# Building fp32 weights from double-precision bits: three VectorE passes after two ScalarE activations, instead of five passes after one

## The chip, the core and the metric

The kernel runs on one core of one Trainium2 chip. The metric is the device time of one execution, in microseconds. A core has five engines that run side by side and wait for one another by semaphores: TensorE (PE, matrix products; its weight loads are PEld), VectorE (DVE), ScalarE (ACT), GpSimd (POOL) and SyncE (SP, which here issues nearly all transfers). Each engine takes its own instructions in order.

## What is computed

An attention block with a delta rule feeds a gated feed-forward block. q, k and v have the shape (4, 8, 768, 48), in single precision; the three weights of the second block are in double precision.

```python
k_n = k / (np.linalg.norm(k, axis=-1, keepdims=True) + 1e-06)
for t in range(S):                       # S = 768
    y[:, :, t] = np.einsum('bhd,bhde->bhe', q[:, :, t], state)
    v_old = np.einsum('bhde,bhd->bhe', state, kt)
    state = state + bt[:, :, :, None] * np.einsum('bhd,bhe->bhde', kt, vt - v_old)
# x = y as 3072 tokens of 384
g = x @ w_gate                           # w_gate, w_val: 384 x 1536, w_out: 1536 x 384
silu = g * (1.0 / (1.0 + np.exp(-g)))
val = x @ w_val
out = (silu * val @ w_out).astype(np.float32)
```

The kernel works through the sequence in 12 chunks of 64 steps. Within a chunk the recurrence is a set of small matrix products and the inverse of a triangular matrix; the first such inverse is a substitution of 31 steps on VectorE, at the start of the kernel. After a chunk's attention part (called `advance`) its 256 tokens (`x_ffn`) go through the feed-forward block: `p_gate` and `p_val` are products with w_gate and w_val, `sil` is the silu of p_gate, `h_f` the product of sil and p_val, `p_o` the product with w_out.

The kernel multiplies in fp32. Each weight arrives as two 32-bit words, and the kernel makes an fp32 number of them. A double's high word holds the sign, 11 bits of exponent and the top 20 bits of mantissa; the low word holds the other 32 bits of mantissa. An fp32 number has 8 bits of exponent and 23 of mantissa.

## The kernel before

The weights are cut into 36 pieces of 128 rows. Pieces 0 to 11 are 256 wide (the first 512 columns of w_gate and w_val in turn, three row blocks each), 12 to 23 are 512 wide (the rest of both), 24 to 35 are 384 wide (w_out). Each piece is loaded into a place that some other tile owns until later (`h_f`, `zt`, `wo_sb`, or `staged`), converted, and only then is its place loaded again. This is the conversion. The L numbers in comments are those by which the profile names the lines; they were added here.

```python
def power_step(n):
    ...
    m = pieces[n][4]
    power = words(hp[10 + (n // 2 % 4 if n < N_HALF else (0, 2, 3, 1)[n % 4])])
    ...
    nc.vector.tensor_scalar(                       # L246: exponent bits of the high word
        out=power, in0=staged[n][:, :, 1],
        scalar1=0x7FF00000, scalar2=None, op0=ALU.bitwise_and,
    )
    nc.scalar.activation(                          # L254: exponent moved and rebiased
        power.bitcast(I32), power, ACTF.Relu, bias=rebias, scale=8.0
    )

def convert(ns):
    ...                                            # power_step for each of ns, if not yet done
    for dst, words, _ in work_of:
        nc.vector.tensor_scalar(                   # L266: top mantissa as an integer
            out=dst.bitcast(U32), in0=words[:, :, 1],
            scalar1=0xFFFFF, scalar2=1 << 20, op0=ALU.bitwise_and, op1=ALU.bitwise_or,
        )
    for dst, words, _ in work_of:
        nc.vector.scalar_tensor_tensor(            # L275: plus the low word, as fp32
            out=dst, in0=words[:, :, 0], scalar=2.0**-32, in1=dst.bitcast(U32),
            op0=ALU.mult, op1=ALU.add,
        )
    for n in range(ns[-1] + 1, ns[-1] + 7):
        if n < min(N_HALF, len(pieces)) or ns[-1] + 3 > n < len(pieces):
            power_step(n)                          # ahead, for later pieces
    for _, words, power in work_of:
        nc.vector.scalar_tensor_tensor(            # L287: the sign into the power of two
            out=power, in0=words[:, :, 1], scalar=0x80000000, in1=power,
            op0=ALU.bitwise_and, op1=ALU.bitwise_or,
        )
    for dst, _, power in work_of:
        nc.vector.scalar_tensor_tensor(            # L296: mantissa times power
            out=dst, in0=dst, scalar=2.0**-20, in1=power.bitcast(FP32),
            op0=ALU.mult, op1=ALU.mult,
        )
    for n in ns:
        for later in freed_by.get(n, ()):
            stage(later)                           # load the next piece into the freed place
```

The order of the start, as the kernel lists it (each engine gets its share in this order):

```python
for n, _ in enumerate(substitute(mb, zb)):   # DVE, L510 and L516
    if n == R // 2:
        for i in range(4):
            power_step(i)
m_1 = turned_m(1, "ffn")
scale_v_heads(0)                             # ACT, L396, 16 small activations
turned(1, True, "px")
for _ in late_z(0, zb):                      # DVE transposes into zt and d_t, L596 and L602
    pass
...
first_join = join_late(0, 0, ("px", "py"))
next(first_join)                             # PE p_j L620, ACT d_o L613 and t L622
converts(2)
next(first_q)                                # DVE p_sb, L459
next(first_join)                             # PE p_j L630, ACT zt L638
nc.scalar.copy(mb[:, m_1[0][0]], m_1[0][1])
step("advance", advance, 0)                  # PE p_u L763, ACT uu L774
converts(2)
step("advance", advance, 0)
nc.scalar.copy(mb[:, m_1[1][0]], m_1[1][1])
converts(2)
step("advance", advance, 0)                  # PE p_y, ACT y L815 and L817
converts(2)
step("advance", advance, 0)                  # PE p_f L827, ACT x_ffn L830
converts(2)
...
converts(2)
...
for c, f in pairs:                           # two 128-wide columns of w_gate and w_val each
    ...
    need((6, 12, 18, 18, 24, 24)[f // 2])    # pieces that must have been issued by then
    gate_val(c, f, fill, 1 if early else None)
need(len(pieces))
for bp in range(NB):
    point(2)
    output(0, bp, fill, (4, 8))              # PE p_o L876
```

`gate_val` issues p_gate (L847), sil (L856), a `fill`, p_val (L847), h_f (L862), a `fill`. While pieces remain, a `fill` converts the next piece (the first three fills the next two, and the first of them one more). `point` puts steps of the next chunk's attention part between: state (ACT L805), the second join (d_o, t, zt on ACT; p_j on PE), p_g (PE L444) and p_sb (DVE L459), p_r and p_y (PE L742, L751), the two passes on vin (DVE L401, L759), p_u (PE L763).

Of the kernel before, what the change touches and what calls it, by code (L numbers as in the profile page):

```python
# [7 lines left out]

FP32 = mybir.dt.float32
U32 = mybir.dt.uint32  # L10
I32 = mybir.dt.int32
ALU = mybir.AluOpType
ACTF = mybir.ActivationFunctionType

# [7 lines left out]
def kernel(  # L22
# [25 lines left out]
    nc = tc.nc  # L48
# [14 lines left out]
    const = ctx.enter_context(tc.tile_pool(name="const", bufs=1))  # L63
# [106 lines left out]
    load_k(0, (nc.sync, nc.scalar))  # L170
    load_k(1, (nc.sync, nc.scalar))
    beta_b = const.tile([128, NG, R], FP32, name="beta_b")
    rebias = const.tile([128, 1], FP32, name="rebias")
    nc.vector.memset(rebias, -896.0 * 2**23)
    wg_sb = const.tile([128, KT, DFF], FP32, name="wg_sb")
    wv_sb = const.tile([128, KT, DFF], FP32, name="wv_sb")
    wo_sb = const.tile([128, FT, DM], FP32, name="wo_sb")
# [3 lines left out]
    pieces = []  # L181
# [9 lines left out]
    staged, powers, places = {}, {}, {}  # L191

    def words(tile_):
        return tile_.bitcast(U32)
# [18 lines left out]
    for n, (name, lo) in enumerate(place_of):  # L213
        m = 2 * pieces[n][4]
# [10 lines left out]
    def stage(n):  # L225
        _, src, t, f0, m = pieces[n]
        name, lo = place_of[n]
        if name not in places:
            tag_bufs = {"zb": 1, "p_sb": 2}[name]
            places[name] = work.tile(  # L230
                [128, 2 * PIECE], U32, name="staged", tag=name, bufs=tag_bufs
            )
        place = places[name][:, lo : lo + 2 * m]
        staged[n] = place.rearrange("p (f two) -> p f two", two=2)
        nc.sync.dma_start(
            out=place, in_=src[t * 128 : (t + 1) * 128, f0 : f0 + m].bitcast(U32)
        )

    def power_step(n):
        if n in powers or n not in staged:  # L240
            return
        m = pieces[n][4]
        power = words(hp[10 + (n // 2 % 4 if n < N_HALF else (0, 2, 3, 1)[n % 4])])
        power = power[:, n % 2 * m : n % 2 * m + m] if n < N_HALF else power[:, 0:m]
        powers[n] = power
        nc.vector.tensor_scalar(  # L246
            out=power,
            in0=staged[n][:, :, 1],
            scalar1=0x7FF00000,
            scalar2=None,  # L250
            op0=ALU.bitwise_and,
        )

        nc.scalar.activation(  # L254
            power.bitcast(I32), power, ACTF.Relu, bias=rebias, scale=8.0
        )

    def convert(ns):

        work_of = []  # L260
        for n in ns:
            dst, _, t, f0, m = pieces[n]
            power_step(n)
            work_of.append((dst[:, t, f0 : f0 + m], staged.pop(n), powers.pop(n)))
        for dst, words, _ in work_of:
            nc.vector.tensor_scalar(  # L266
                out=dst.bitcast(U32),
                in0=words[:, :, 1],
                scalar1=0xFFFFF,
                scalar2=1 << 20,  # L270
                op0=ALU.bitwise_and,
                op1=ALU.bitwise_or,
            )
        for dst, words, _ in work_of:
            nc.vector.scalar_tensor_tensor(  # L275
                out=dst,
                in0=words[:, :, 0],
                scalar=2.0**-32,
                in1=dst.bitcast(U32),
                op0=ALU.mult,  # L280
                op1=ALU.add,
            )
        for n in range(ns[-1] + 1, ns[-1] + 7):
            if n < min(N_HALF, len(pieces)) or ns[-1] + 3 > n < len(pieces):
                power_step(n)
        for _, words, power in work_of:
            nc.vector.scalar_tensor_tensor(  # L287
                out=power,
                in0=words[:, :, 1],
                scalar=0x80000000,  # L290
                in1=power,
                op0=ALU.bitwise_and,
                op1=ALU.bitwise_or,
            )
        for dst, _, power in work_of:
            nc.vector.scalar_tensor_tensor(  # L296
                out=dst,
                in0=dst,
                scalar=2.0**-20,
                in1=power.bitcast(FP32),  # L300
                op0=ALU.mult,
                op1=ALU.mult,
            )
        for n in ns:
            for later in freed_by.get(n, ()):
                stage(later)
# [10 lines left out]
    for b in range(2):  # L317
        rows = mask_q[64 * b : 64 * b + 64]
        nc.gpsimd.affine_select(
            out=rows,  # L320
# [688 lines left out]
    def converts(n):  # L1009
        if todo:  # L1010
            convert(todo[:n])
            del todo[:n]
# [121 lines left out]
    with tc.manual_schedule(  # L1134
# [17 lines left out]
        for n in range(4):  # L1152
            stage(n)
# [3 lines left out]
        for n in range(4, 10):  # L1157
            stage(n)
# [32 lines left out]
        for n, _ in enumerate(substitute(mb, zb)):  # L1191
# [3 lines that stand above are left out]
# [102 lines left out]
```

## Time and profile before

| what | value |
|---|---|
| time, median of 3 runs | 738.45 us (738.15 to 738.98) |
| span of the profiled execution | 737.5 us |
| TensorE busy | 697.5 us, 95% |
| weight loads of TensorE busy | 604.7 us, 82% |
| VectorE busy | 473.1 us, 64% |
| ScalarE busy | 154.7 us, 21% |
| GpSimd busy | 66.9 us, 9% |
| bytes read from device memory | 31.01 MB |

The busy share is an average over stages with different limits, so it is read by stage: a line of 40 digits gives the busy tenths of each slice of 18.4 us, and a table of stretches gives busy microseconds. A timeline lists instructions by start time; the tile that is written stands left of the arrow, the tiles read right of it, then the shape and the count; a bracket at the end gives how long the engine had been idle before it and which instruction ended that. "Busy" counts an instruction's whole duration, and neighbours on VectorE and ScalarE overlap a little, so what one costs in a row is read from start to start. Conversions run from 33.6 us (the first L246) to 141 us (the last L296).

### The profile page before, as it was taken

What the parts mean: (1) busy time and instruction counts of PE and PEld (TensorE: products, weight loads), DVE (VectorE), ACT (ScalarE), POOL (GpSimd) and SP (SyncE); (2) the same over time, 40 slices, a digit from 0 to 9 for tenths busy, and PEclk for the clock granted to TensorE, in tenths of its full rate; (3) what the DMA queues carried; (4) which work ended last, traced back from release to release, by engine and by line L of the source; (5) the groups of instructions that cost most, each with busy time, mean ns of one, the idle gap of its engine ahead of it and who ended that gap; (6) DMA issues with size and microseconds to landing.
All of it is one profiled execution on the core that took longest, in us unless ns stands there. A gap on an engine that the chain in (4) does not pass through costs nothing.

```text
span 737.5 us, 22478 instructions
## 1 busy us (share of the span) xinstructions
PE 697.5 (95%) x10132; PEld 604.7 (82%) x10132; DVE 473.1 (64%) x977; ACT 154.7 (21%) x287; POOL 66.9 (9%) x46
## 2 busy tenths in 40 slices
PE   4657899999999999999999999999999999999997
PEld 3546788866787788988988988988988988989987
DVE  5999988978498163678854678854578853313122
ACT  3455443302401112011012011012011012021010
POOL 7008100201200000030000030000030000000000
PEclk9556999999999999999999999999999999999999
DMA  6775444121231012331302231302210100100000
GB/s 141 164 227 166 124 108 129 36 41 24 56 45 24 22 24 45 43 67 15 53 3 45 36 70 20 53 3 39 46 29 12 32 3 3 23 3 0 22 1 21
DMA packets 130735, 37.18 MB, mean 50 GB/s; under 512 B 122864, under 2 KB 125936, under 8 KB 130640
## 3 DMA queue, kind: packets, MB, share of 16 engines
q1 hardware_dynamic: 127184, 34.01, 22.7%
q10 hardware_dynamic: 3072, 1.57, 1.0%
q8 instruction: 79, 1.29, 0.7%
q0 software_dynamic: 384, 0.17, 0.1%
q14 instruction: 16, 0.13, 0.1%
HBM read 31.01 MB, written 4.72 MB: 48 GB/s over the span
## 4 chain that ended last, share of the span: by engine, by line
PE 83%; DVE 14%; issue 1%; DMA 1%; ACT 0%; ACTq 0%; SPq 0%; DVEq 0%
PE p_gate L847 23%; PE p_val L847 23%; PE p_o L959 17%; PE p_o L876 6%; DVE tmp L510 3%; PE p_g L444 3%; DVE zb L516 3%; PE p_u L763 2%; PE p_r L742 1%; PE p_s L794 1%; PE p_y L782 1%; PE p_y L751 1%; DVE last_h L287 1%; PE p_t L432 1%; DVE h_f L862 1%
## 5 line engine op out<-in xcount | busy, mean ns | idle before, releaser
L847 PE MATMUL p_gate<-x_ffn,wg_sb 128*128 128x256 f32 x864 | 204.4, 387 | 1.5 <-ACT x_ffn L830 1.5
L847 PE MATMUL p_val<-x_ffn,wv_sb 128*128 128x256 f32 x864 | 198.5, 379 | 0.0
L847 PEld LDWEIGHTS p_val<-x_ffn,wv_sb 128*128 128x128 f32 x864 | 163.8, 190 | 22.3
L847 PEld LDWEIGHTS p_gate<-x_ffn,wg_sb 128*128 128x128 f32 x864 | 161.1, 191 | 24.2 <-ACT x_ffn L830 2.0
L862 DVE TENSOR_TENSOR h_f<-sil,p_val 128x512 f32<-128x512 f32 x71 | 48.6, 684 | 147.5 <-PE p_val L847 147.0
L856 ACT ACTIVATE sil<-p_gate 128x512 f32<-128x512 f32 x72 | 43.0, 598 | 276.9 <-PE p_gate L847 247.3
L655 POOL TENSOR_TENSOR n_b<-mb,half 128x32 f32<-128x32 f32 x5 | 43.0, 8607 | 408.6 <-DVE mb L480 368.2
L959 PE MATMUL p_o<-wo_sb,h_f 128*128 128x192 f32 x432 | 75.6, 328 | 0.1
L959 PEld LDWEIGHTS p_o<-wo_sb,h_f 128*128 128x128 f32 x432 | 70.3, 190 | 1.2 <-DVE o_sb L969 0.7
L510 DVE TENSOR_TENSOR tmp<-zb,mb 128x31 f32<-128x31 f32 (+15 forms) x186 | 63.3, 340 | 12.2 <-PE p_j L630 6.8
L516 DVE TENSOR_TENSOR zb<-zb,tmp 128x31 f32<-128x31 f32 (+15 forms) x186 | 63.7, 343 | 6.5 <-DVE tmp L510 0.2
L969 DVE TENSOR_TENSOR o_sb<-o_sb,p_o 128x192 f32<-128x192 f32 x45 | 15.8, 350 | 53.4 <-PE p_o L959 36.2
L876 PE MATMUL p_o<-wo_sb,h_f 128*128 128x384 f32 x136 | 45.7, 490 | 0.0
L876 PEld LDWEIGHTS p_o<-wo_sb,h_f 128*128 128x128 f32 x136 | 25.3, 190 | 16.5
L959 PE MATMUL p_o<-last_k,h_f 128*128 128x192 f32 x180 | 32.2, 326 | 0.0
L959 PEld LDWEIGHTS p_o<-last_k,h_f 128*128 128x128 f32 x180 | 29.7, 190 | 0.0
L917 DVE TENSOR_TENSOR h_f<-h_f,h_f 128x256 f32<-128x256 f32 x54 | 22.4, 424 | 8.0 <-PE p_o L959 7.1
L959 PE MATMUL p_o<-last_h,h_f 128*128 128x192 f32 x144 | 26.3, 326 | 0.0
L959 PEld LDWEIGHTS p_o<-last_h,h_f 128*128 128x128 f32 x144 | 23.9, 190 | 0.0
L254 ACT ACTIVATE last_h<-last_h,rebias 128x512 int32<-128x512 uint32 (+2 forms) x26 | 15.3, 616 | 30.5 <-DVE last_h L246 30.4
L763 PEld LDWEIGHTS p_u<-vin,zt 64*64 64x64 f32 x768 | 13.7, 141 | 6.9 <-issue 3.2
L763 PE MATMUL p_u<-vin,zt 64*64 64x48 f32 x768 | 15.7, 228 | 2.4 <-DVE vin L759 1.2
(180 smaller groups left out, 692.6 us busy)
## 6 DMA issues: line engine op xcount, KB each, us to landing
vin<-in_v_dram SPq DMA_DIRECT2D x96, 48.0 KB
kn<-in_k_dram SPq DMA_DIRECT2D x40, 96.0 KB
out_dram<-o_sb SPq DMA_DIRECT2D x36, 96.0 KB
zt<-in_moe_w_out_dram SPq DMA_DIRECT2D x6, 384.0 KB
staged<-in_moe_w_out_dram SPq DMA_DIRECT2D x6, 384.0 KB
qpad<-in_q_dram SPq DMA_DIRECT2D x36, 64.0 KB
wo_sb<-in_moe_w_gate_dram SPq DMA_DIRECT2D x4, 512.0 KB
wo_sb<-in_moe_w_val_dram SPq DMA_DIRECT2D x4, 512.0 KB
```

Source lines behind the costliest of these rows:

```text
L444: nc.tensor.matmul(p_v[par][half_of(b if of_q else b ^ par), bp, j], kt[c][half_of(par), bp, j, b], xt[half_of(par), bp, j, b],)
L510: nc.vector.tensor_tensor(out=t_v, in0=zb[:, 0 : j + 1, j : j + 1].to_broadcast([128, j + 1, m]), in1=mb[:, j : j + 1, j + 1 : R].to_broad ...
L516: nc.vector.tensor_tensor(out=zb[:, 0 : j + 1, j + 1 : R], in0=zb[:, 0 : j + 1, j + 1 : R], in1=t_v, op=ALU.add,)
L655: nc.gpsimd.tensor_tensor(out=n, in0=mb.rearrange("p j i -> p (j i)")[:, 0 : R * R : R + 1], in1=half, op=ALU.pow,)
L763: nc.tensor.matmul(p_u[half_of(b), par, bp, j], zt[half_of(b ^ par), par, bp, j], r[half_of(b ^ par), par, bp, j], start=first, stop=True, ...
L847: nc.tensor.matmul(ps[name][:, i], w_sb[:, t, (f + i) * 128 : (f + i + 1) * 128], xts[c][:, t], start=(t == 0), stop=(t == KT - 1),)
L856: nc.scalar.activation(sil, ps[name], ACTF.Silu)
L862: nc.vector.tensor_tensor(out=hs[c, f], in0=sil, in1=ps["p_val"], op=ALU.mult)
L876: nc.tensor.matmul(p_o, hs[c, f - f % 2][:, f % 2, bp * 128 : (bp + 1) * 128], wo_sb[:, f], start=(f == 0), stop=(f == FT - 1),)
L917: nc.vector.tensor_tensor(out=out, in0=a, in1=b, op=ALU.subtract)
L959: nc.tensor.matmul(p[x, part], a(f - f % 2)[:, f % 2], b(f), start=not begun and f == 0, stop=f == FH - 1, skip_group_check=True,)
L969: nc.vector.tensor_tensor(out=out, in0=a, in1=b, op=ALU.add)
```

## The change

The exponent and the top mantissa are no longer taken apart. ScalarE reads the high word as if it were an fp32 number: its 8 exponent bits are then the upper 8 of the double's 11, and the lower 3 stand at the top of the mantissa. Multiplying by 2^-112 subtracts 112 from that exponent, so that a shift left by 3 then gives the exponent and the upper mantissa of the wanted fp32 number in place. A second activation multiplies the low word by 2^-29 and rounds it to an integer from 0 to 8: the last three bits of the mantissa, rounded. VectorE shifts the first result by three, puts the sign back (it lay in the bit that the shift pushed out), and adds the second result as an integer. So ScalarE has two activations per piece where it had one, with constants instead of a bias read from memory, and neither waits for a VectorE pass on the same piece; VectorE has three passes where it had five. The shifted words go to the piece's own place, over its first half. The order of pieces, the places, and the loads are as they were. It is for taking work off VectorE in the stage where the weights are converted.

```diff
-    rebias = const.tile([128, 1], FP32, name="rebias")
-    nc.vector.memset(rebias, -896.0 * 2**23)
...
-        staged[n] = place.rearrange("p (f two) -> p f two", two=2)
+        staged[n] = place
...
     def power_step(n):
...
-        nc.vector.tensor_scalar(
-            out=power,
-            in0=staged[n][:, :, 1],
-            scalar1=0x7FF00000,
-            scalar2=None,
-            op0=ALU.bitwise_and,
+        words_of = staged[n].rearrange("p (f two) -> p f two", two=2)
+        nc.scalar.activation(
+            dst[:, t, f0 : f0 + m],
+            words_of[:, :, 1].bitcast(FP32),
+            ACTF.Copy,
+            scale=2.0**-112,
         )
-
-        nc.scalar.activation(
-            power.bitcast(I32), power, ACTF.Relu, bias=rebias, scale=8.0
-        )
+        nc.scalar.activation(power, words_of[:, :, 0], ACTF.Copy, scale=2.0**-29)
 
     def convert(ns):
...
-        for dst, words, _ in work_of:
+            place = staged.pop(n)[:, 0:m]
+            work_of.append((dst[:, t, f0 : f0 + m].bitcast(U32), place, powers.pop(n)))
+        for dst, place, _ in work_of:
             nc.vector.tensor_scalar(
-                out=dst.bitcast(U32),
-                in0=words[:, :, 1],
-                scalar1=0xFFFFF,
-                scalar2=1 << 20,
+                out=place,
+                in0=dst,
+                scalar1=3,
+                scalar2=None,
+                op0=ALU.logical_shift_left,
+            )
+        for dst, place, _ in work_of:
+            nc.vector.scalar_tensor_tensor(
+                out=dst,
+                in0=dst,
+                scalar=0x80000000,
+                in1=place,
                 op0=ALU.bitwise_and,
                 op1=ALU.bitwise_or,
-            )
...                                          (the mult-add with the low word goes)
         for n in range(ns[-1] + 1, ns[-1] + 7):
             if n < min(N_HALF, len(pieces)) or ns[-1] + 3 > n < len(pieces):
                 power_step(n)
...                                          (the pass that set the sign in power goes)
         for dst, _, power in work_of:
...                                          (the product with the power goes)
+            nc.vector.tensor_tensor(out=dst, in0=dst, in1=power, op=ALU.add)
         for n in ns:
             for later in freed_by.get(n, ()):
                 stage(later)
```

More of the change, by code (lines that the diff above doesn't have):

```diff
@@ L10 @@
 U32 = mybir.dt.uint32
-I32 = mybir.dt.int32
 ALU = mybir.AluOpType
@@ L241, in power_step @@
             return
-        m = pieces[n][4]
+        dst, _, t, f0, m = pieces[n]
         power = words(hp[10 + (n // 2 % 4 if n < N_HALF else (0, 2, 3, 1)[n % 4])])
@@ L263, in convert @@
             power_step(n)
-            work_of.append((dst[:, t, f0 : f0 + m], staged.pop(n), powers.pop(n)))
-        for dst, words, _ in work_of:
+            place = staged.pop(n)[:, 0:m]
+            work_of.append((dst[:, t, f0 : f0 + m].bitcast(U32), place, powers.pop(n)))
+        for dst, place, _ in work_of:
             nc.vector.tensor_scalar(
-                out=dst.bitcast(U32),
-                in0=words[:, :, 1],
-                scalar1=0xFFFFF,
-                scalar2=1 << 20,
+                out=place,
[10 more added lines that the diff above has]
+                in1=place,
                 op0=ALU.bitwise_and,
                 op1=ALU.bitwise_or,
-            )
[L274 to L281, printed above, removed]
             )
@@ L285, in convert @@
                 power_step(n)
[L286 to L294, printed above, removed]
-        for dst, _, power in work_of:
[L296 to L303, printed above, removed]
+        for dst, _, power in work_of:
+            nc.vector.tensor_tensor(out=dst, in0=dst, in1=power, op=ALU.add)
         for n in ns:
```

## The prediction

> **What bounds the kernel now.** I read the busy slices first, then busy time by stretches of 20 us, then the timeline of each engine between 28 and 145 us beside the chain of waits. Of the slices (40 of 18.4 us) the lines for TensorE, VectorE, ScalarE and the granted clock:
>
> ```profile
> PE   4657899999999999999999999999999999999997
> DVE  5999988978498163678854678854578853313122
> ACT  3455443302401112011012011012011012021010
> PEclk9556999999999999999999999999999999999999
> ```
>
> From the sixth slice (92 us) on TensorE is at 90% or more; VectorE is full only in the first five. The same by stretches (columns: length; busy us and count of TensorE, its weight loads, VectorE, ScalarE, GpSimd; clock; DMA share; GB/s):
>
> ```profile
> 40.00:60.00 20.00, 11.22 (x345) 9.37 (x344) 19.45 (x60) 10.73 (x23) 1.58 (x1) 0.50 0.71 212
> 60.00:80.00 20.00, 15.84 (x305) 12.80 (x309) 19.93 (x48) 12.21 (x24) 16.62 (x1) 0.82 0.71 190
> 80.00:100.00 20.00, 18.39 (x440) 15.84 (x441) 18.29 (x33) 7.15 (x12) 0.00 (x0) 1.00 0.28 72
> 100.00:120.00 20.00, 20.00 (x220) 17.69 (x219) 16.90 (x37) 8.71 (x17) 0.00 (x0) 1.00 0.49 136
> ```
>
> VectorE has 0.6 us free between 40 and 80 us; from 100 us TensorE has none. So a shorter conversion can pay only before about 92 us, and only where TensorE waits. One pair of 512-wide pieces on VectorE (timeline: start, duration, line):
>
> ```profile
> 65.63 0.44 DVE L266 TENSOR_SCALAR wg_sb<-wo_sb 128x512 uint32<-128x512 uint32 x1
> 65.97 0.44 DVE L266 TENSOR_SCALAR wv_sb<-wo_sb 128x512 uint32<-128x512 uint32 x1
> 66.31 0.70 DVE L275 SCALAR_TENSOR_TENSOR wg_sb<-wo_sb,wg_sb 128x512 f32<-128x512 uint32 x1
> 66.91 0.70 DVE L275 SCALAR_TENSOR_TENSOR wv_sb<-wo_sb,wv_sb 128x512 f32<-128x512 uint32 x1
> 67.51 0.77 DVE L246 TENSOR_SCALAR last_h<-wo_sb 128x512 uint32<-128x512 uint32 x2
> 68.18 0.70 DVE L287 SCALAR_TENSOR_TENSOR h_f<-wo_sb,h_f 128x512 uint32<-128x512 uint32 x1
> ...
> 69.38 0.70 DVE L296 SCALAR_TENSOR_TENSOR wg_sb<-wg_sb,h_f 128x512 f32<-128x512 f32 x1
> ```
>
> Neighbours overlap, so the cost is start to start: 0.34 us for a one-input pass, 0.60 for a two-input pass. In the same timeline a 256-wide piece has 0.20 and 0.335, a 384-wide one 0.27 and 0.47. What TensorE waits for between 60 and 92 us stands in brackets in its timeline (length, releaser):
>
> ```profile
> 64.04 4.46 PE L847 MATMUL p_gate<-x_ffn,wg_sb 128*128 128x256 f32 x12 [0.95 <-ACT x_ffn L830]
> ...
> 74.24 0.24 PE L630 MATMUL p_j<-ident,d_o 32*32 32x32 f32 x2 [0.95 <-ACT d_o L613]
> ...
> 79.88 1.16 PE L444 MATMUL p_g<-qt,kt 64*64 64x64 f32 x64 [0.28 <-ACT zt L638]
> ...
> 85.29 1.15 PE L751 MATMUL p_y<-state,qt 64*64 64x48 f32 x64 [0.39 <-DVE p_sb L459]
> ...
> 90.45 1.15 PE L763 MATMUL p_u<-vin,zt 64*64 64x48 f32 x64 [1.23 <-DVE vin L759]
> ```
>
> The first p_gate starts when x_ffn is there, at the end of a TensorE and ScalarE chain (p_j, zt, p_u, uu, p_y, y, p_f, x_ffn) that begins with VectorE's transposes at 44.75 us. After it TensorE idles 0.95 + 0.42 (a second wait for d_o) + 0.28 + 0.39 + 1.23 = 3.27 us until p_u, all behind VectorE: two waits for it directly, and ScalarE is late with d_o because its L254 at 72.12 us had waited 1.76 us for L246.
>
> [...] The built program shows the new integer add as one instruction over 512 elements for a 256-wide piece, so over 16-bit halves[...]. L254, which has such a bias, takes 0.505, 0.614 and 0.716 us at 256, 384 and 512[...]. [...] L275 reads every second word and takes 0.434 us at 256, as dense L296 does.
>
> **The change part by part.** Removed from VectorE per piece: one one-input pass (L246) and one two-input pass (of L275, L287, L296, two stay as sign and add; of L246 and L266 one stays as the shift). At 512: 2.48 becomes 0.34 + 0.60 + 0.60 = 1.54 us, 0.94 less; at 256: 1.405 becomes 0.87, 0.535 less; at 384: 1.95 becomes 1.21, 0.74 less. With 12 pieces of each, VectorE loses 12 x (0.535 + 0.94 + 0.74) = 26.6 us. ScalarE gets two activations with immediate scales for one with a bias pointer: [...] 0.31, 0.41, 0.52 us each against L254's 0.40, 0.52, 0.63 start to start, so 12 x (0.22 + 0.30 + 0.41) = 11.2 us more. They no longer wait for VectorE, but VectorE's first pass now waits for both a landed piece and ScalarE.
>
> Before x_ffn: the four L246 in the middle of the first substitution (33.62 to 34.43 us) leave VectorE's chain, so its transposes come 0.81 us earlier. ScalarE then has eight activations between t and zt: 8 x 0.31 = 2.5 us, in a gap of 3.3 us (49.5 to 52.8). Two more pieces stand before uu and two before y: 0.35 us more each, against idle times of 0.41 us there. I take 0.1 us of delay in all: first p_gate at 63.35, 0.7 earlier.
>
> VectorE meanwhile: 12 small pieces at 0.87 are 10.4 us, plus p_sb 1.2, from 47.0 to 58.6; but pieces 12 and 13 stand on ScalarE behind x_ffn, so they come at 64.4 and 65.4. VectorE idles several us here, where it was full before. That is why most of its gain is lost before TensorE sees it.
>
> From there with the trace's durations. First p_gate ends 67.8, silu 68.4. ScalarE: pieces 14 to 16, 3 x 1.04, to 71.5; state 0.78, d_o 1.3, t 0.4, to 74.0 (before: 75.26). TensorE resumes p_j and starts the second p_gate at 75.5 (76.74). ScalarE: pieces 17 and 18 to 76.1, zt 2.3 to 78.4; p_gate ends 78.3, p_g starts 78.5 (79.88). p_val ends 82.35, p_r 83.45. VectorE: h_f at 72.3 to 73.0, pieces 15 and 16 to 76.1, 17 and 18 to 79.2, p_sb after p_g to 80.9, so p_y needs no wait at 83.5 and the third p_gate runs to 87.35. VectorE: h_f to 83.0, piece 19 alone (three dependent passes, 1.54 + 0.2) to 84.8, the two vin passes 2.0 to 86.8: p_u needs no wait and starts at 87.4, 3.05 us before 90.45. The parts: 0.7 from the substitution, 0.55 less waiting for d_o, 0.25 of the wait for zt, 0.4 for p_sb and 1.2 for vin make 3.1 us. After p_u TensorE is full in both kernels; the other 11 to 13 us taken off VectorE lie beside it and are worth nothing. 738.45 - 3.1 = 735.3.
>
> **Rivals.** ScalarE becomes the bound: d_o (L613) reads with a wide hop and takes 0.639 us for 256 elements[...]. Should every-second-word reads cost the same, eight activations would take 4.4 us in a gap of 3.3, x_ffn would come about 1 us later than I say, d_o 2.8 us later: 737.5 to 740. VectorE's reads of two-word hops at full rate speak against it. The add runs one half per cycle: then 512 words are a two-input pass of 1024, which takes 1.22 us (L497), and VectorE still needs 2.07 against 2.48 us, and its margin at vin (0.55 us) is used up: about 736. The whole gain shows: the chain of waits names VectorE nearly without a break from 17.4 to 90.4 us, and the pieces done by then save some 15 us, which would mean 723; TensorE's own work, idle only 3.3 us after 64 us, excludes it. Transfers take the place: a new piece is loaded only once VectorE has read the old one, and silu stands behind activations that wait for landing. Before, the reuse took some 4.1 us from issue to first read (107.5 to 111.7). A wait of 1 us would still be covered, since TensorE needs a silu only after two later products; at worst the gain is halved: 737.
>
> **Range and chances.** The waits that can vanish cap the gain at 0.8 + 3.3 = 4.1 us (734.3), or slightly more if the start shifts; the first rival sets the other end. So 733.9 to 737.3, most likely 735.3. Two per cent are 14.8 us, far outside all of these but the excluded one: 0.01 faster, 0.98 within, 0.01 slower.
>
> **What will show it.** VectorE busy about 26 to 30 us below 473.1, ScalarE about 14 above 154.7 (activation durations, overlaps counted twice); the add at about 0.43, 0.56, 0.70 us for the three widths; activations at 0.40, 0.51, 0.61; VectorE idle around 60 us behind ScalarE; the first p_gate near 63.3 and the first p_u of the second chunk near 87.4 without a wait for vin; the rest of the trace shifted and otherwise alike. Wrong if activations take over 0.5 us at 256, if the first p_gate is not earlier, or if TensorE waits anew after 92 us.

## The result, and the profile after

| | before | changed |
|---|---|---|
| time, median | 738.72 us (738.15 to 740.21, 4 runs) | 736.18 us (735.33 to 736.6, 4 runs) |
| ratio to before | | 0.9958, 95% interval 0.9943 to 0.9974 |
| VectorE busy | 473.1 us | 447.2 us |
| ScalarE busy | 154.7 us | 167.4 us |
| TensorE busy | 697.5 us | 696.3 us |
| span of the profiled execution | 737.5 us | 733.5 us |

The change takes 25.9 us off VectorE's busy time, puts 12.7 us on ScalarE, and the kernel is about 0.4% faster: by the ratio 3.1 us, with an interval of 1.9 to 4.2 (the medians differ by 2.5). The two profiled executions differ by 4.0 us, more than the times do: their starts were not alike (the first step of the substitution came at 20.69 us before and at 19.83 after, though the change touches nothing ahead of it but one small memset; in the twelve profiles of all kernels it lies between 19.27 and 20.78 us, and no run shows why). So stages are compared below by their lengths, not by when they come.

The busy slices of the changed kernel (40 of 18.3 us), as for the kernel before:

```profile
PE   4757999999999999999999999999999999999997
DVE  5995756797597252769853678853678853313122
ACT  3567664202401102021012021012021012021010
PEclk9557999999999999999999999999999999999999
```

VectorE was at 90% or more from the second slice to the fifth; now it has room from the fourth on, and ScalarE is at six or seven tenths from the third to the sixth. TensorE reaches 90% one slice earlier. In stretches of 20 us (columns as before):

```profile
40.00:60.00 20.00, 10.62 (x329) 8.84 (x328) 17.75 (x51) 13.90 (x35) 3.78 (x1) 0.50 0.68 179
60.00:80.00 20.00, 17.60 (x367) 14.35 (x366) 13.21 (x24) 16.50 (x30) 1.85 (x1) 0.87 0.83 225
80.00:100.00 20.00, 20.00 (x391) 17.30 (x390) 12.66 (x21) 9.55 (x18) 0.00 (x0) 1.00 0.29 63
100.00:120.00 20.00, 20.00 (x220) 17.68 (x219) 12.36 (x26) 10.33 (x21) 0.00 (x0) 1.00 0.40 120
```

Between 60 and 80 us VectorE went from 19.93 busy microseconds to 13.21, ScalarE from 12.21 to 16.50. A pair of 512-wide pieces on VectorE (timeline), six passes for ten:

```profile
71.59 0.42 DVE L261 TENSOR_SCALAR wo_sb<-wv_sb 128x512 uint32<-128x512 uint32 x1
71.92 0.42 DVE L261 TENSOR_SCALAR zt<-wg_sb 128x512 uint32<-128x512 uint32 x1
72.26 0.68 DVE L269 SCALAR_TENSOR_TENSOR wv_sb<-wv_sb,wo_sb 128x512 uint32<-128x512 uint32 x1
72.86 0.68 DVE L269 SCALAR_TENSOR_TENSOR wg_sb<-wg_sb,zt 128x512 uint32<-128x512 uint32 x1
73.46 0.68 DVE L281 CUSTOM_DVE_ANT_0 wv_sb<-wv_sb,last_h 128x1024 uint16<-128x1024 uint16 x1
74.06 0.68 DVE L281 CUSTOM_DVE_ANT_0 wg_sb<-wg_sb,h_f 128x1024 uint16<-128x1024 uint16 x1
...
```

From start to start that is 0.33, 0.34, 0.60, 0.60, 0.60 and 0.61 us: L261 is the shift, L269 sets the sign, L281 is the integer add, over 1024 halves of 16 bits. TensorE's timeline between the first p_gate and p_u of the second chunk, to be held against the same five places before:

```profile
61.84 4.56 PE L825 MATMUL p_gate<-x_ffn,wg_sb 128*128 128x256 f32 x12 [0.95 <-ACT x_ffn L808]
...
71.82 0.24 PE L608 MATMUL p_j<-ident,d_o 32*32 32x32 f32 x2 [0.65 <-ACT d_o L591]
72.48 0.21 PE L608 MATMUL p_j<-ident,d_o 32*32 32x32 f32 x1 [0.42 <-ACT d_o L591]
...
77.56 1.16 PE L422 MATMUL p_g<-qt,kt 64*64 64x64 f32 x64 [0.39 <-ACT zt L616]
...
82.41 1.11 PE L729 MATMUL p_y<-state,qt 64*64 64x48 f32 x64
...
86.24 1.15 PE L741 MATMUL p_u<-vin,zt 64*64 64x48 f32 x64
```

Both waits that named VectorE (for p_sb, 0.39 us, and for vin, 1.23 us) are gone. The three that name ScalarE (d_o twice, zt) are still there, 1.46 us together. VectorE idles where the prediction put it, behind ScalarE (its timeline):

```profile
62.93 0.43 DVE L261 TENSOR_SCALAR wo_sb<-wg_sb 128x512 uint32<-128x512 uint32 x1 [3.82 <-ACT h_f L250]
64.04 0.43 DVE L261 TENSOR_SCALAR wo_sb<-wv_sb 128x512 uint32<-128x512 uint32 x1 [0.69 <-ACT last_h L250]
```

### The profile page after: what moved, and what is told of

It is laid out like the page before. It is cut to its first block, busy times and chain, and to the rows that moved or that the text cites. A ratio compares the mean times of both kernels' runs of the same rounds, so it can differ in the third digit from the quotient of the medians.

```text
span 733.5 us, 22491 instructions
## 1 busy us (share of the span) xinstructions
PE 696.3 (95%) x10132; PEld 603.8 (82%) x10132; DVE 447.2 (61%) x904; ACT 167.4 (23%) x323; POOL 54.2 (7%) x46
## 3 DMA queue, kind: packets, MB, share of 16 engines
q8 instruction: 79, 1.29, 0.8%
## 4 chain that ended last, share of the span: by engine, by line
PE 84%; DVE 9%; ACT 4%; issue 2%; POOL 1%; DMA 1%; ACTq 0%; SPq 0%; DVEq 0%
PE p_gate L825 24%; PE p_val L825 23%; PE p_o L937 17%; PE p_o L854 6%; PE p_g L422 3%; DVE tmp L488 3%; DVE zb L494 3%; PE p_u L741 2%; PE p_r L720 2%; PE p_s L772 1%; PE p_y L760 1%; PE p_y L729 1%; POOL n_t L343 1%; PE p_f L805 1%; ACT last_h L250 1%
## 5 line engine op out<-in xcount | busy, mean ns | idle before, releaser
L633 POOL TENSOR_TENSOR n_b<-mb,half 128x32 f32<-128x32 f32 x5 | 30.5, 6091 | 408.2 <-DVE mb L458 369.7
L458 DVE STREAM_TRANSPOSE mb<-a_sb 32x1024 f32<-32x1024 f32 x8 | 17.1, 2139 | 0.2
```

The lines of the kernel that those rows point to most:

```text
L458: nc.vector.transpose(out(rows, 0), in_(rows, 0))
L633: nc.gpsimd.tensor_tensor(out=n, in0=mb.rearrange("p j i -> p (j i)")[:, 0 : R * R : R + 1], in1=half, op=ALU.pow,)
```

## The experiments

Four lengths are read from the profile of every kernel: **A**, from the first step of the substitution to VectorE's transpose into zt; **B**, from there to the first p_gate; **C**, from there to p_u of the second chunk; **D**, from that p_u to the first p_o. A + B + C is the stage that the change can shorten.

| kernel | A | B | C | A+B+C | D |
|---|---|---|---|---|---|
| before | 24.06 | 19.29 | 26.41 | 69.76 | 59.40 |
| before, again | 24.05 | 18.18 | 27.51 | 69.74 | 59.40 |
| new in pieces 24 to 35 alone | 24.05 | 18.48 | 27.22 | 69.75 | 59.39 |
| new in pieces 0 to 3 alone | 23.35 | 20.62 | 27.49 | 71.46 | 59.40 |
| new in pieces 4 to 23 alone | 24.05 | 18.69 | 25.53 | 68.27 | 59.39 |
| changed | 23.36 | 18.65 | 24.40 | 66.41 | 59.40 |
| changed, again | 23.37 | 19.30 | 24.64 | 67.31 | 59.40 |
| changed, a third time | 23.38 | 18.66 | 24.35 | 66.39 | 59.39 |
| changed, copies halved between two engines | 23.39 | 19.92 | 24.08 | 67.39 | 59.39 |
| before, with the same halving | 24.06 | 21.38 | 31.64 | 77.08 | 59.39 |
| changed, copies shared by PSUM tile | 23.38 | 17.88 | 23.24 | 64.50 | 59.40 |
| before, with the same sharing | 24.05 | 18.46 | 31.05 | 73.56 | 59.39 |

**Which pieces bring the gain (four kernels).** The theory: the gain comes from the first four pieces (the substitution) and from the pieces up to p_u; the last twelve lie beside a full TensorE. The rival: every piece counts, so the last twelve bring their share. In three of the kernels, the pieces outside a set are converted in the old way:

```diff
+    NEW = range(0, 4)        # or range(4, 24), or range(24, 36)
     def power_step(n):
...
+        if n not in NEW:
+            ...              # L246 and L254 of the kernel before
+            return
     def convert(ns):
...
+            if n in NEW:     # three passes, as changed
...
+            else:            # the other four passes of the kernel before
```

The changed kernel itself once more:

> The changed kernel once more, as it is, so that the partial versions sent with it have the whole change beside them on the same chip. 0.9958 x 738.7 = 735.6 us, 2.5 to 3.5 us under the kernel before. In its trace the first p_gate should again start about 0.8 to 1.5 us earlier against the start of the substitution than before (43.35 us after it before, 42.0 in the first trace of the changed kernel), and the next p_u about 24.4 us after that p_gate (before 26.4).

Measured: 736.78 us (735.73 to 738.34, 9 runs) against 738.53 for before on the same chip, ratio 0.9978 (0.9968 to 0.9988). The gain is 0.9 to 2.4 us here, less than the 2.5 to 3.5 expected, and 1.9 to 4.2 in the first comparison; they overlap at 1.9 to 2.4. The first p_gate came 42.67 us after the start of the substitution, 0.7 us earlier than before and just short of the expected 0.8.

Pieces 0 to 3 alone:

> Only pieces 0 to 3 are built in the new way, 4 to 35 in the old. My theory (only what stands in VectorE's chain before the first p_gate, or delays what TensorE waits for until 92 us, counts): the four exponent passes leave the first substitution, 0.81 us, and VectorE's later work hardly changes, so 0.6 to 1.0 us faster than before. Rival theory A (VectorE's work counts wherever it lies until 92 us, as the chain of waits suggests): the four pieces save 4 x 0.535 = 2.1 us. Rival theory B (the substitution isn't on the path, all gain comes from the later waits): no difference.

Measured: 737.82 us, ratio 0.999 (0.9982 to 0.9999): 0.7 us, between 0.1 and 1.3. Length A is 0.71 us shorter, and 0.7 shorter in every kernel with new pieces 0 to 3, in none of the others. Rival A's 2.1 us falls by the interval, and rival B's zero only just; it is length A that speaks against B. (The long A+B+C of this profile is taken up below.)

Pieces 4 to 23 alone:

> Only pieces 4 to 23 are built in the new way; the four exponent passes stay in the substitution, and pieces 24 to 35 stay old. My theory: the TensorE waits between the first p_gate and p_u shrink as with the whole change (2.0 us of the 3.3), the substitution keeps its length, so 1.7 to 2.4 us faster than before. Rival A: VectorE's saving by 92 us, 8 x 0.535 + 9 x 0.94 = 12.7 us, would show as 12 us. Rival B: 2.5 to 3.1 us, the whole gain.

Measured: 736.72 us, ratio 0.9977 (0.9969 to 0.9985): 1.8 us, between 1.1 and 2.3, so the theory's 1.7 to 2.4 stands, and both rivals (12 us, and 2.5 to 3.1) fall. A is as before, and A+B+C is 1.5 us shorter (with a first p_gate of 5.49 us, 0.9 more than in the first profile of the changed kernel; of this below).

Pieces 24 to 35 alone:

> Only pieces 24 to 35 (w_out) are built in the new way: VectorE loses 12 x 0.74 = 8.9 us between 100 and 141 us, ScalarE gains 12 activations there. My theory: TensorE has no wait there, so no difference from before, within 0.4 us. Rival C (VectorE's share counts everywhere in proportion): a third of the gain, 1 us. Rival D (activations that wait for landed pieces stand in front of silu and hold up TensorE): slower by 0.5 us or more.

Measured: 739.1 us, ratio 1.0009 (1.0001 to 1.0018), so no gain, but 0.6 us more, where no difference over 0.4 was expected. The trace has no place for it: A+B+C and D are those of before to 0.01 us, and the median span on the core is 736.8 us for both kernels. The difference stands outside the span: time less span is 2.21 us in this kernel, 1.72 before, 1.90 in the changed kernel. So rival C falls. The 0.6 us is the size that rival D gave, but D's reason does not hold, since A+B+C and D are not longer. The expectation missed some tenths of a microsecond ahead of or behind the program's work, the cause of which is not known.

In the median spans, 0.7 us (pieces 0 to 3), 1.8 (4 to 23) and 0.0 (24 to 35) stand against 1.9 for all together. That the parts give 2.5 us is no contradiction: by the intervals the first two are 0.1 to 1.3 and 1.1 to 2.3 us, and the whole 0.9 to 2.4.

**What sets p_u (two runs).** The theory: before, VectorE's own work sets p_u, so A+B+C doesn't vary, whatever TensorE does ahead of it; after, TensorE's and ScalarE's chain sets it, so TensorE's pauses count.

> The kernel before once more, for the scatter of its stages. From the first step of the substitution to p_u of the second chunk it took 69.76 us. Theory: VectorE sets p_u, and takes up what TensorE's own delays vary by, so this is 69.76 again within 0.1 us, whenever the first p_gate comes. Rival: TensorE's chain sets it, and it varies by 0.5 us or more.

Measured: 739.4 us once; A+B+C is 69.74 us, and it is 69.75 in the kernel with new pieces 24 to 35 alone, whose first 24 pieces are the old ones. In TensorE's timeline, among the small products p_j, there is a pause that nothing in the profile explains (its releaser is given as "issue"). It was 1.38 us in the first profile of before

```profile
51.23 0.26 PE L630 MATMUL p_j<-ident,d_o 32*32 32x32 f32 x2 [1.38 <-issue]
```

and 0.28 here (the line numbers are those of the mixed kernels):

```profile
50.19 0.26 PE L665 MATMUL p_j<-ident,d_o 32*32 32x32 f32 x2 [0.28 <-issue]
...
63.01 5.49 PE L882 MATMUL p_gate<-x_ffn,wg_sb 128*128 128x256 f32 x12 [0.95 <-ACT x_ffn L865]
...
90.52 1.15 PE L798 MATMUL p_u<-vin,zt 64*64 64x48 f32 x64 [0.88 <-DVE vin L794]
```

So B is 1.1 us shorter here, and nothing of it is left at p_u. The first p_gate took 5.49 us and not 4.46: twelve such products take 5.49 us while the clock granted to TensorE (a share of its full speed) is 0.5, and 2.86 at 1.0 (the next p_gate, at 76.74 us in the first profile), and the clock rose later here. In the stretch of 67 to 68 us the clock was 0.84 in the first profile of before, and 0.50 here (the column before the last two):

```profile
67.00:68.00 1.00, 1.00 (x5) 0.83 (x5) 1.00 (x4) 0.00 (x0) 1.00 (x1) 0.84 0.68 184
67.00:68.00 1.00, 1.00 (x4) 0.67 (x2) 1.00 (x4) 0.00 (x0) 1.00 (x1) 0.50 0.88 356
```

Between 76 and 80 us it was 0.57 here once more (1.00 in the first). TensorE was busy longer from the end of p_gate to p_u, and its waits on the way fell from 3.27 to 2.01 us; p_u came at the same place. In both profiles it starts 0.05 to 0.06 us after VectorE has written vin, and from 34 us up to that point VectorE has no gap over 0.15 us in either. So VectorE sets p_u there. The single waits of one profile are no fixed costs: here TensorE waited neither for zt nor for p_sb.

> The changed kernel once more, for the same stretch: 66.41 and 67.31 us were seen. Theory: p_u now stands at the end of TensorE's and ScalarE's chain, so the stretch from the substitution to p_u varies with the pauses of TensorE among the small products p_m and p_j, between 66 and 68 us, and nearly all of what it varies by lies between the transposes into zt and the first p_gate. Rival: VectorE still sets it: the same within 0.1 us as one of the two.

Measured: 735.78 us once; A+B+C is 66.39 us. The same lines of TensorE's timeline in this third profile of the changed kernel:

```profile
48.95 0.26 PE L608 MATMUL p_j<-ident,d_o 32*32 32x32 f32 x2 [0.30 <-issue]
...
62.22 4.49 PE L825 MATMUL p_gate<-x_ffn,wg_sb 128*128 128x256 f32 x12 [0.95 <-ACT x_ffn L808]
...
86.57 1.15 PE L741 MATMUL p_u<-vin,zt 64*64 64x48 f32 x64
```

and in the second:

```profile
49.64 0.26 PE L608 MATMUL p_j<-ident,d_o 32*32 32x32 f32 x2 [1.39 <-issue]
...
62.46 4.79 PE L825 MATMUL p_gate<-x_ffn,wg_sb 128*128 128x256 f32 x12 [0.95 <-ACT x_ffn L808]
...
87.10 1.15 PE L741 MATMUL p_u<-vin,zt 64*64 64x48 f32 x64
```

With pauses of 0.57, 0.30 and 1.39 us the changed kernel takes 66.41, 66.39 and 67.31 us to p_u; the kernel before takes 69.76 and 69.74 with 1.38 and 0.28. VectorE no longer sets p_u, as the theory has it, though by little: vin is written 0.22 us before p_u starts in all three. In exchange TensorE's own delays now cost time. Of the 0.9 us between the profiles 0.65 is B, most and not nearly all of it. The rest is the first p_gate, which took 4.56, 4.49 and 4.79 us (in the first of the three the clock was 0.50 up to 65 us, 0.84 from 65 to 66 and 1.00 after that): C less this p_gate is 19.84, 19.86 and 19.85 us. Only part of the pause reaches B: with 0.30 and 0.57 us B is the same, because ScalarE's eight activations ahead of zt, 2.6 us long, hold it for longer than that.

The scatter of the whole spans does not decide the matter: its standard deviation is 0.37 us in 37 runs of before and 0.72 in 9 of the changed kernel, but 0.81 in 10 runs of before on another chip. The kernel with new pieces 0 to 3 had a pause of 4.68 us among the products p_m, and TensorE was done with them at 44.83 us, 2.2 after the start of the transpose into zt (before: 43.06, 1.7 ahead of it). A long B would follow from that; the execution was 1.5 us over the kernel's median, so its A+B+C is not typical.

**Is there room on VectorE now (four kernels)?** If so, copies that ScalarE makes on the way to the first p_gate can go to VectorE and bring more; in the kernel before, the same move must cost time. The first attempt halved each copy of the first chunk between the engines, within one PSUM tile (of the edit, two of the four copies):

```diff
-            for hi in (QUADS[0][0], QUADS[2][0]):
-                nc.scalar.copy(zt_v[hi, e], p_j[hi, e])
+                nc.scalar.copy(zt_v[QUADS[0][0], e], p_j[QUADS[0][0], e])
+            for e in range(2):
+                nc.vector.tensor_copy(zt_v[QUADS[2][0], e], p_j[QUADS[2][0], e])
...
+        copy = lambda bp: nc.vector.tensor_copy if bp == 1 else nc.scalar.copy
         for bp in each:
-            nc.scalar.copy(uu[:, :, bp], p_u[:, :, bp])
+            copy(bp)(uu[:, :, bp], p_u[:, :, bp])
...          (y, x_ffn alike; the second join's d_o on VectorE, ahead of the first p_gate)
```

> The changed kernel, with the room that it left on VectorE used: half of each PSUM copy of the first chunk (zt, uu, y, x_ffn) and the copy d_o of the second join move from ScalarE to VectorE. The theory (after the change TensorE and ScalarE, not VectorE, set when p_u of the second chunk starts): zt 0.9 us, y 1.1 us and x_ffn 0.4 us shorter, so the first p_gate comes 2 to 2.5 us sooner after VectorE's transpose into zt; the waits for d_o (1.07 us) and for zt (0.39 us) go; p_u 3 to 4 us earlier than in the changed kernel, and the time 3 to 4 us under its 736.8: about 733.2. The rival (VectorE is still the bound, and the change only moved its work): 5.4 us of copies more on VectorE before p_u make vin late, and the time is no better than 736.8, or worse by up to 3 us.

Measured: 735.72 us, ratio 0.9956 (0.9943 to 0.997). That is 1.1 us under the 736.78 of the changed kernel, not 3 to 4, with intervals that overlap. At the same pause (1.40 us) A+B+C is 67.39 us against 67.31, but the first p_gate took 5.49 us for 4.79, which is its length at a clock of 0.5 in the second profile of before. Without it the stretch is 61.90 us for 62.52, 0.6 less: B is 0.6 us longer, and C less its p_gate 1.3 shorter (18.59 for 19.85), since the waits for d_o are gone. The theory's number fails, and the rival is not excluded: p_u starts 0.06 us after vin is written, the distance that it has where TensorE waits for vin, so VectorE is at its limit there again. Why B did not become shorter stands in VectorE's timeline:

```profile
52.34 1.29 DVE L622 COPY zt<-p_j 32x512 f32<-32x512 f32 x2 [1.44 <-ACT zt L619]
...
56.15 0.56 DVE L763 COPY uu<-p_u 128x384 f32<-128x384 f32 x1 [1.27 <-ACT uu L763]
...
59.19 0.36 DVE L804 COPY y<-p_y 128x192 f32<-128x192 f32 x1 [0.68 <-ACT y L806]
...
62.49 0.56 DVE L819 COPY x_ffn<-p_f 128x384 f32<-128x384 f32 x1 [0.34 <-ACT x_ffn L819]
```

Each of VectorE's halves starts only after ScalarE's half, not after the product: by the profile's releasers the second reader waits for the first, and the halves ran one after the other. Even the two halves of zt, which lie in different partitions (VectorE waited 1.44 us), and those of x_ffn, which lie in the two 512-wide halves of one tile (0.34 us), did so. Why the readers are ordered no run here shows.

> The same edits in the kernel before. The theory: VectorE has no room there between 40 and 90 us, so the 5.4 us of copies that it takes over, less its 1.2 us of waiting for p_sb and the like, come on top: vin ends 3 to 6 us later, TensorE waits that much longer for it at p_u, and the time is 741.5 to 744.5, although the first p_gate comes earlier or no later. If the copies had merely been badly shared, whichever conversion is used, it would gain 3 us here too: 735.5.

Measured: 746.34 us, ratio 1.0103 (1.0089 to 1.0116): 7.4 us slower, A+B+C 77.08 us, 7.3 more. The direction is the theory's, the size is above its range. The copies are 5.5 us by the durations of the changed kernel's variant (2 x 1.29 + 0.56 + 1.08 + 0.56 + 0.76); the pieces that were converted singly, not in pairs, are a likely part of the rest, which was not measured by itself.

The second attempt avoids sharing a PSUM tile: both d_o copies of the first two joins go to VectorE whole, zt is copied in two instructions and not four, and p_y of the first chunk lies in two tiles, one for each engine:

```diff
+        copy_d = nc.vector.tensor_copy if g == 0 else nc.scalar.copy
         for s in range(2):
-            nc.scalar.copy(d_o[QUADS[2 * s + 1][0]], d_v[QUADS[2 * s][0], 1])
+            copy_d(d_o[QUADS[2 * s + 1][0]], d_v[QUADS[2 * s][0], 1])
...
+        if g == 0:
+            for hi in (QUADS[0][0], QUADS[2][0]):
+                nc.scalar.copy(zt_v[hi], p_j[hi])
...
+        if c == 0:
+            p_y = [... for p in banks("p_y", "ffn")]     # two tiles of their own
...
+        copy = nc.vector.tensor_copy if c == 0 else nc.scalar.copy
+        nc.scalar.copy(y[:, :, :, 0], p_y[0])
+        for b in range(2):
+            copy(y[half_of(b), :, :, 1], p_y[1][half_of(1 - b)])
...          (the second join's d_o ahead of the first p_gate, as in the first attempt)
```

> The changed kernel with copies shared so that neither engine waits for the other's reading of one PSUM tile: for the first two chunks both d_o copies go to VectorE (0.76 us each, 1.29 on ScalarE), zt is copied in two instructions of 1024 elements and not four of 512 (2.0 for 2.36 us), and p_y of the first chunk lies in two single PSUM tiles, of which ScalarE copies one (0.5 us) and VectorE the other (1.0 us), 1.0 in place of 2.0 us. Theory (after the change p_u of the second chunk stands behind TensorE's and ScalarE's chain): the first p_gate 1.5 to 2 us earlier after VectorE's transpose into zt, the waits for d_o (1.07 us) gone, p_u 2.5 to 3.3 us earlier, the time 2.3 to 3.3 us under the changed kernel: about 733.5 to 734.5. Rival (VectorE still sets p_u): its 2.5 us more of copies are lost again, 736.5 to 738.

Measured: 732.59 us (731.91 to 733.7), ratio 0.9911 (0.9896 to 0.9927): 6.3 us under the kernel before, and 3.6 and 4.2 us under the two medians of the changed kernel, more than the 2.3 to 3.3 expected. With a pause of 1.37 us, A+B+C is 64.50 us, 2.8 less than in the changed kernel with 1.39, although the first p_gate took 0.5 us longer (5.31 for 4.79). B is 1.4 us shorter, C less its p_gate 1.9. The two parts of y, still interleaved in one SBUF tile but read from two PSUM tiles, now run side by side, ScalarE's

```profile
57.31 0.48 ACT L807 COPY y<-p_y 128x384 f32<-128x384 f32 x1
```

and VectorE's, of which the releaser is TensorE:

```profile
46.27 0.78 DVE L592 COPY d_o<-d_t 32x256 f32<-32x256 f32 x2
...
57.35 1.12 DVE L809 COPY y<-p_y 64x384 f32<-64x384 f32 x2 [3.75 <-PE p_y L774]
```

In TensorE's timeline the wait for y is 1.36 us (2.07 in the changed kernel), and the waits for d_o and for zt after the first p_gate are gone; p_u still has none for vin:

```profile
58.62 1.51 PE L819 MATMUL p_f<-ident,y 128*128 128x128 f32 x6 [1.36 <-DVE y L809]
61.08 5.31 PE L839 MATMUL p_gate<-x_ffn,wg_sb 128*128 128x256 f32 x12 [0.95 <-ACT x_ffn L822]
...
75.64 1.16 PE L422 MATMUL p_g<-qt,kt 64*64 64x64 f32 x64
...
84.32 1.15 PE L755 MATMUL p_u<-vin,zt 64*64 64x48 f32 x64
```

> The same edits in the kernel before. Theory (VectorE sets p_u there, with 0.6 us free between 40 and 80 us): d_o twice and half of y are 2.5 us more on VectorE, p_u comes that much later behind vin: 740 to 741.5. If sharing the copies were worth as much without the change, 735 to 736.

Measured: 741.67 us, ratio 1.0032 (1.0019 to 1.0044): 2.8 us slower, at the upper end of what was expected, and A+B+C 3.8 us longer (the start, which A+B+C leaves out, was 1.1 us shorter in this profile than in the first of before). B was shorter than in the first profile of before, by 0.8 us, and it helped nothing; TensorE waits for vin at p_u, as before:

```profile
93.12 1.15 PE L777 MATMUL p_u<-vin,zt 64*64 64x48 f32 x64 [1.23 <-DVE vin L773]
```

The same edits gain about 4 us in the changed kernel and lose 2.8 in the one before. So the room on VectorE is real, and the change alone did not use it. How much of the gain each of the edits brings is not shown; the copy of zt in two instructions (2.03 us for 2.36) needs no room on VectorE.

## Why the prediction was right, and where it was off

The time was predicted at 735.3 us and measured at 736.18 and 736.78, within the range. By its own steps:

- **VectorE's passes.** 0.34 and 0.60 us start to start at 512: measured 0.33 to 0.34 and 0.60 to 0.61. 26.6 us less in all: 25.9 less busy time. The add, predicted at 0.43, 0.56 and 0.70 us, took 0.41 to 0.42, 0.56 and 0.68 to 0.69. That the add would cost a word what the other two-input passes do was the author's estimate; it did (L269: 0.41, 0.56 and 0.68 to 0.69), and the rival, by which 512 words take the 1.22 us of a pass over 1024, falls.
- **ScalarE's activations.** Predicted durations of 0.40, 0.51 and 0.61 us, the author's estimates (in the trace of before a scaling activation took 0.38 us at 256, L622, a copy 0.48 at 384, L774, and silu 0.60 at 512, L856; neighbours of L254 overlapped by about 0.1), measured 0.41 to 0.46, 0.53 to 0.57 and 0.66 to 0.70; start to start about 0.33, 0.44 and 0.57 for 0.31, 0.41 and 0.52. By these durations an element costs 0.94 ns ((0.67 - 0.43) us / 256), which leaves 0.19 us of the 0.43 at 256 (both estimates). The rival by which eight activations take 4.4 us falls: between t and zt the eight took 2.6. Busy time rose by 12.7 us, predicted 14.
- **Before x_ffn.** Transposes 0.81 us earlier were predicted, and they came 0.68 to 0.70 earlier in the three profiles. "0.1 us of delay in all" in B holds only where the pause among the p_j was long: with 1.38 and 1.39 us B is 19.29 before and 19.30 after, and the first p_gate comes 0.68 earlier (0.7 predicted). With 0.28 and 0.30 B is 18.18 before and 18.66 after, so the first p_gate gains only 0.2. The gap of 3.3 us into which the prediction puts ScalarE's eight activations held the pause. In the second profile of before it is 2.2 us (t ends at 49.58, zt starts at 51.74); in the third of the changed kernel the eight take 2.6 us, and zt starts right behind them:

```profile
48.35 0.43 ACT L244 ACTIVATE wg_sb<-h_f 128x256 f32<-128x256 f32 x1
...
50.65 0.41 ACT L250 ACTIVATE last_h<-h_f 128x256 uint32<-128x256 uint32 x1
50.98 2.36 ACT L616 COPY zt<-p_j 32x512 f32<-32x512 f32 x4
```

  So the rival that has ScalarE as the bound is right here by half a microsecond, with activations near the predicted cost (2.5 us for the eight).
- **VectorE idle near 60 us.** Seen: 3.82 us, and 0.69 more. TensorE waits meanwhile for y and x_ffn (2.07 and 0.95 us), which are ScalarE's copies.
- **From the first p_gate to p_u.** Predicted 24.05 us, measured 24.40, 24.64 and 24.35, of which the first p_gate has 0.10, 0.33 and 0.03 more than the 4.46 us taken over from before. Against the first profile of before the terms for p_sb (0.4) and vin (1.2) came as said, with 0.22 us to spare at vin where 0.55 was reckoned. Those for d_o and zt did not: "0.55 less waiting for d_o" was 0.3 less (1.37 us before, 1.07 after), and "0.25 of the wait for zt" was a wait longer by 0.1 (0.28 before, 0.39 after). This is the step that fell short, and its size was that of the activations: ScalarE stands between silu and d_o with six of them, 512 wide. Its timeline in the changed kernel:

```profile
66.43 0.60 ACT L834 ACTIVATE sil<-p_gate 128x512 f32<-128x512 f32 x1 [2.43 <-PE p_gate L825]
66.93 0.66 ACT L244 ACTIVATE wg_sb<-wo_sb 128x512 f32<-128x512 f32 x1
...
69.78 0.66 ACT L250 ACTIVATE h_f<-zt 128x512 uint32<-128x512 uint32 x1
70.34 0.78 ACT L783 COPY state<-p_s 128x768 f32<-128x768 f32 x1
71.14 1.29 ACT L591 COPY d_o<-d_t 32x256 f32<-32x256 f32 x2
```

  The six take 66.93 to 70.34, 3.41 us, where the prediction had 3 x 1.04 = 3.12; four more ahead of zt take 2.33 us (72.86 to 75.19) for 2.08. Together that is 0.54 us, nearly the 0.6 by which these two terms fell short.
- **The sum.** 3.05 us to p_u was predicted. The profiles with short pauses give 3.35 and 3.37, the one with the long pause 2.45; by the ratios of the times it was 3.1 and 1.6 us. The mechanism holds: VectorE gives up p_u, and what TensorE and ScalarE need sets the gain. That the number is near is in part luck. The prediction took the gap ahead of zt and the 4.46 us of the first p_gate as fixed, but both vary from one execution to the next, and only while VectorE sets p_u does that cost nothing. With the long pause and a first p_gate of 5.49 us the lengths above would add up to 68.0 us (an estimate: 23.37 + 19.30 + 5.49 + 19.85), 1.75 less than before. The three profiled executions of the changed kernel (735.33, 735.78 and 736.20 us) all lie below the median of nine, 736.78.
- **After p_u nothing.** D is 59.39 to 59.40 us in all twelve profiles, with VectorE's load in it as before or eased. The rival of the whole gain (723 us) falls, and so does that of transfers: ScalarE waits for landing pieces at 103.30, 122.31 and 127.85 us (0.96, 0.45 and 0.80 us), and TensorE doesn't wait for ScalarE there.

## What to carry to other kernels

Work taken off a full engine is worth only what the next bound leaves: here 26 us less on VectorE became 1.6 to 3.1, since ScalarE's copies and TensorE stood right behind it, and everything after 87 us was TensorE's already. The rest of the gain is room, and room has to be used: moving copies onto the freed engine brought about 4 us more, though the same move into the kernel before cost 2.8. A full VectorE also hid the delays of the others here: in the three profiles with the old pieces up to p_u A+B+C was 69.74 to 69.76 us, with pauses of 0.28 to 1.38 us and a first p_gate of 4.46 to 5.49 us. Once VectorE no longer set p_u, the pause and the p_gate showed in it (66.39 to 67.31 us). Where two engines read halves of one PSUM tile, they ran one behind the other here (VectorE waited 0.34 to 1.44 us for ScalarE's half); with a tile each they ran side by side (starts at 57.31 and 57.35 us).

## What the runs showed beyond that

- The integer add of 32-bit words is built as an add over twice as many 16-bit halves and took 0.41 to 0.42, 0.56 and 0.68 to 0.69 us for 256, 384 and 512 words; the pass that sets the sign, of two inputs too, took 0.41, 0.56 and 0.68 to 0.69.
- The copy of d_o with its wide hop took 1.29 us for two on ScalarE (changed kernel) and 0.78 for two on VectorE (copies shared by PSUM tile).
- TensorE paused among the same small products p_j for 0.28 to 1.65 us from one execution to the next, and for 1.92 to 5.23 us among the p_m, with no releaser in the profile.
- In the first profiles of the two kernels the clock rose from 0.50 to 1.00 during the first p_gate (0.84 from 67 to 68 us before, from 65 to 66 us with the change). Its twelve products took 4.46 to 5.49 us in the twelve profiles, and in two of them the second p_gate was long as well: 4.13 us in the second profile of before, where the clock was 0.57 once more, and 5.36 in the kernel before with the halving, for 2.86 at 1.0. What sets the clock no run here shows.
- Time outside the span differs by kernel (1.72 us before, 1.88 to 1.90 with the change, 2.21 with the change in the last twelve pieces alone), so some tenths of a microsecond of a comparison are in no part of a trace.
